# First batch of an attention and mixture kernel: second scores by blocks of 32 tokens, with the queries as the stationary side, and a new written order

## The chip, the core and the metric

The kernel runs on one core of a Trainium2 chip. TensorE multiplies (its weight loads are listed as PEld), VectorE (DVE), ScalarE (ACT) and GpSimd (POOL) work element by element, and SyncE (SP) issues the transfers. The metric is the device time in microseconds. The kernel before takes 466.59 us (median of 3 runs, 466.55 to 466.61).

## The reference

```python
batch, n_heads, seq, head_dim = (8, 8, 576, 64)      # p: 32 rows
def sm_attn(qq, kk, vv):
    s = scale * np.matmul(qq, kk.transpose(0, 1, 3, 2))
    s = s - np.max(s, axis=-1, keepdims=True)
    a = np.exp(s)
    a = a / (np.sum(a, axis=-1, keepdims=True) + 1e-09)
    return np.matmul(a, vv)
p_packed = sm_attn(p, k, v)
out = sm_attn(q, p_packed, p_packed)
...
h = np.maximum(np.maximum(x @ w1, x @ w2), x @ w3)
return (h @ w_out).astype(np.float32)
```

For every batch and head, 32 learned rows p attend to 576 keys (first scores); the 32 packed rows that come out are keys and values for the 576 queries (second scores, over 32 columns). The heads' outputs, side by side, are the tokens x of a layer with three 512 x 768 weights, a maximum over the three products, and a 768 x 512 output weight.

## The kernel before

The work of one batch is cut into steps named by a letter. `S` computes the first scores (`scores`), `A` their softmax and, for batches 0 and 1, the transposition on TensorE (`weigh_and_turn`), `Z` the inverse sums, `V` the values, `K` the packed rows, transposed into `pt_sb`, `Q` the second scores (`queries`), `B` their softmax (`attend`). From batch 2 on `X` (`spread`) stands for the transposition on TensorE: VectorE transposes 32 x 32 blocks (line 313), and 16 small transfers that SyncE issues (line 319) put the blocks in place. The packed rows aren't multiplied with the second softmax: `P` (`project`) multiplies them with the three weights of a group j of 128 columns, and `N` (`layer_in`) multiplies that with the softmax, which is layer 1. High and low parts of both operands, three products, stand in for full precision, so that one (j, half, weight) takes 6 matmuls of 288 columns. `E` takes the maximum over the weights, `H` prepares layer 2's operands, `O` is layer 2 (`layer_out`), `F` sums and stores. `k`, `v`, `q`, `w` are loads; `C` (`convert`) turns a weight block as it lies in memory into numbers: two steps on ScalarE (lines 188 and 193), a shift on VectorE (202), an addition on GpSimd (206). `W` prepares the output weight.

The order is written by hand, or by a program that printed it: the string `START` holds batches 0 and 1 and the beginning of batch 2, and the string `LOOP` one round for each batch from 2 on. Each word advances its step to the next `yield`; a last letter v, g or a moves that piece to VectorE, GpSimd or ScalarE. Each engine, SyncE too, takes its instructions in the order that the words give, and waits at one whose input isn't there. `I` and `J` are filler matmuls on an identity (`rouse`, line 143), by number of 128 columns.

Two heads share the 128 partitions of `q` (parities r = 0 and 1, 64 dimensions each), and a batch has four such pairs (`QUADS`). In `queries` the packed rows are stationary, so the scores come out with 32 packed rows of each pair as partitions and 288 tokens (a half, hf) as columns:

```python
nc.tensor.matmul(
    out=s2[b][hf][32 * n:32 * n + 32, r, 0:HS],
    lhsT=pt_sb[b % 2][o, NP * n:NP * n + NP], rhs=q[g][o, pr, hf * HS:(hf + 1) * HS],
```

`attend` therefore first transposes blocks of 32 x 32 on VectorE (line 389), so that a token's 32 scores lie in a row, then takes the maximum (393), subtracts (395), exponentiates (ScalarE, 397), sums (400), adds 1e-9 (403 or 405), inverts (407), multiplies (409), transposes back (412), and makes the high part (`a2h`, 415) and the low part (`a2l`, 418). In batch 0 it does so in four pieces of 288 columns, one for each parity and half (words `B000` to `B011`: batch, parity, half); later batches in two pieces of 576.

TensorE's tiles lie in PSUM: `ps_big` has two buffers of two banks (scores, projections), `ps_moe` four of one (layer 1, layer 2, filler). A buffer is given on when its last reader is done.

Of the kernel before, what the change touches and what calls it, by code (L numbers as in the profile page):

```python
# [10 lines left out]
F32 = mybir.dt.float32  # L11
# [21 lines left out]
NT = S // NP  # L33
# [55 lines left out]
def fused_kernel(ctx: ExitStack, tc: tile.TileContext, kp, qt, va, vb, wi, wo, out):  # L89
# [33 lines left out]
    def on(default):  # L123
        return engine[chosen[0] or default]
# [13 lines left out]
    def rouse(ps):  # L138

        k = ps.shape[-1] // P  # L140
        for i in range(0, idle[0], k):
            n = min(idle[0] - i, k)
            nc.tensor.matmul(  # L143
                out=ps[:, 0:n * P], lhsT=ident, rhs=ident.unsqueeze(1).to_broadcast([P, n, P]),
                start=True, stop=True,
            )
        idle[0] = 0
# [208 lines left out]
    def queries(b):  # L356

        q = [loaded["q", b, g] for g in range(G)]
        s2[b] = []
        for hf in range(2):  # L360
            s2[b].append(ps_big.tile([P, R, 512], F32, name=f"s2_{b}_{hf}", tag="big"))
            rouse(s2[b][hf][:, 0])
            for n, (g, pr) in enumerate(QUADS):
                for r in range(R):
                    o = slice(64 * r, 64 * r + 64)
                    nc.tensor.matmul(  # L366
                        out=s2[b][hf][32 * n:32 * n + 32, r, 0:HS],
                        lhsT=pt_sb[b % 2][o, NP * n:NP * n + NP], rhs=q[g][o, pr, hf * HS:(hf + 1) * HS],
                        start=True, stop=True,
                    )  # L370
            if b == 0 or hf == 1:
                yield 0

    def attend(b, r, hf=None):

        parts = range(2) if hf is None else (hf,)
        n = HS * len(parts)
        c = slice(parts[0] * HS, parts[0] * HS + n)
        nt = n // NP

        def buffer(name, dtype=F32):
            if (name, b, r) not in loaded:
                loaded[name, b, r] = pool.tile([P, S], dtype, name=f"{name}{b}_{r}", tag="y", bufs=NY)
            return loaded[name, b, r][:, c]


        e = buffer("e")
        for x in parts:
            nc.vector.transpose(out=e[:, x * HS - c.start:(x + 1) * HS - c.start], in_=s2[b][x][:, r, 0:HS])
        e3 = e.rearrange("p (t x) -> p t x", x=NP)  # L390
        yield 1
        m = pool.tile([P, nt], F32, name=f"m2_{b}_{r}_{c.start}", tag="m2", bufs=4)
        nc.vector.tensor_reduce(out=m, in_=e3, axis=AX.X, op=ALU.max)
        yield 0
        on("g").tensor_tensor(out=e3, in0=e3, in1=m.unsqueeze(2).to_broadcast([P, nt, NP]), op=ALU.subtract)
        yield 2
        nc.scalar.activation(out=e, in_=e, func=AF.Exp, scale=SCALE)
        yield 1
        z = pool.tile([P, nt], F32, name=f"z2_{b}_{r}_{c.start}", tag="z2", bufs=4)
        nc.vector.tensor_reduce(out=z, in_=e3, axis=AX.X, op=ALU.add)  # L400
        yield 0
        if on("a") is nc.scalar:
            nc.scalar.activation(out=z, in_=z, func=AF.Copy, bias=1e-9)
        else:
            nc.vector.tensor_scalar_add(out=z, in0=z, scalar1=1e-9)
        yield 0
        nc.vector.reciprocal(out=z, in_=z)
        yield 0
        on("v").tensor_tensor(out=e3, in0=e3, in1=z.unsqueeze(2).to_broadcast([P, nt, NP]), op=ALU.mult)
        yield 1  # L410
        et = buffer("et")
        nc.vector.transpose(out=et, in_=e)
# [6 lines left out]
        a2[b, r] = loaded["a2h", b, r], loaded["a2l", b, r]  # L419


    pw = {}
# [36 lines left out]
    def layer_in(b, j):  # L459

        p_hi, p_lo = pw[b, j]
        first = b == 0 and j == 0
        for hf in range(2):
            c = slice(hf * HS, (hf + 1) * HS)
            for i in range(NW):
                new = (range(NW) if i == 0 else ()) if first else (i,)
                for x in new:
                    sums[b, j, hf, x] = ps_moe.tile([P, 512], F32, name=f"mi{b}_{j}_{hf}_{x}", tag="moe")
                rouse(sums[b, j, hf, i])

                steps = [((2 * i + x) % 3, (2 * i + x) // 3) for x in range(2)] if first else [(i, 0), (i, 1)]
                for x, r in steps:
                    a_hi, a_lo = a2[b, r]
                    for n, (w, a) in enumerate(((p_hi, a_hi), (p_lo, a_hi), (p_hi, a_lo))):
                        nc.tensor.matmul(  # L475
                            out=sums[b, j, hf, x][:, 0:HS], lhsT=w[:, r, x * P:(x + 1) * P], rhs=a[:, c],
                            start=(r == 0 and n == 0), stop=(r == R - 1 and n == 2),
                        )
                yield 0
# [125 lines left out]
    def weigh_and_turn(b, r):  # L605
# [3 lines left out]


    stages = {
        "S": scores, "A": weigh_and_turn, "Z": invert, "X": spread, "V": lambda b, *rs: values(b, rs), "K": packed, "Q": queries,
        "B": attend, "C": convert, "P": project, "N": layer_in, "E": maximum, "H": halves,
        "O": layer_out, "F": finish, "W": weights,
    }
    loads = {"k": load_k, "v": load_v, "q": load_q, "w": load_w}
# [75 lines left out]
```

## Time and profile before

The table is from one profiled execution of the kernel before.

| | |
|---|---|
| median of the runs | 466.59 us |
| the profiled execution | 466.18 us |
| its span | 464.4 us |
| matmul instructions busy | 455.2 us (98%) |
| VectorE, GpSimd, ScalarE busy | 333.5, 247.9, 159.9 us |
| bytes read and written | 41.94 and 9.44 MB |

Lines of the chain of waits give a start, a length and what ran: `PE s L366` are the second scores, `PE s L253` the first, `PE mi L475` layer 1, `PE idle L143` filler, `DMA q<-in_qt` a load of q that was waited for. Rows of groups give busy time, mean ns of one, and the idle time before it with what ended it. Rows of a timeline give start, length, and how many instructions were merged. SPq is SyncE issuing. A matmul of plain 32-bit floats is two records. Matmul ends are modelled, so a busy matmul engine isn't one at its peak.

### The profile page before, as it was taken

The numbers are of one execution on the slowest core, as the hardware profiler recorded it, in microseconds if no ns is written. First come the engines' busy times: TensorE is split into PE (matmuls) and PEld (weight loads), VectorE is DVE, ScalarE is ACT, GpSimd is POOL, SyncE is SP. The second block draws the span as 40 slices with busy tenths as digits, with TensorE's granted clock in tenths as the row PEclk, the third lists the DMA queues.
The fourth block names the chain that finished last, engine by engine and source line by source line (L and its number), as shares of the span: only waits on it lengthen the run. The fifth ranks groups of instructions, "written<-read, shape, count | busy, mean of one in ns | idle before, by whom it ended". The sixth has DMA issues, their size and how long they took to land.

```text
span 464.4 us, 11561 instructions
## 1 busy us (share of the span) xinstructions
PE 455.2 (98%) x4724; PEld 404.9 (87%) x4724; DVE 333.5 (72%) x698; ACT 159.9 (34%) x341; POOL 247.9 (53%) x213
## 2 busy tenths in 40 slices
PE   7999998999999999999999999999999999999996
PEld 3477887899899898998899988998989988998996
DVE  1799987888887678566887479766786668845552
ACT  2787856535322126022331025121260223302130
POOL 0468875574542675526572384706764275725832
PEclk9999999999999999999999999999999999999999
DMA  8999846010316430256004450065202540020002
GB/s 313 398 382 355 321 98 230 1 58 25 95 66 195 135 119 1 80 160 233 2 27 152 87 211 2 27 199 155 94 1 94 151 116 1 28 76 1 2 6 97
DMA packets 35780, 55.66 MB, mean 120 GB/s; under 512 B 17296, under 2 KB 26512, under 8 KB 35728
## 3 DMA queue, kind: packets, MB, share of 16 engines
q1 hardware_dynamic: 35728, 54.93, 35.4%
q8 instruction: 37, 0.61, 0.5%
q14 instruction: 15, 0.12, 0.1%
HBM read 41.94 MB, written 9.44 MB: 111 GB/s over the span
## 4 chain that ended last, share of the span: by engine, by line
PE 88%; DMA 5%; SPq 3%; DVE 3%; issue 1%; ACT 1%; DVEq 0%
PE mi L475 44%; PE mo L544 29%; PE pw L439 6%; PE idle L143 2%; SPq L319 2%; PE s L366 2%; PE av L337 2%; DMA wi<-in_wi 2%; PE s L253 2%; DMA q<-in_qt 1%; DMA kt<-in_kp 1%; PE tp L296 0%; DMA xt<-x 0%; SPq L159 0%; PE pa L337 0%
## 5 line engine op out<-in xcount | busy, mean ns | idle before, releaser
L475 PE MATMUL mi<-a2h,ph 128*128 128x288 f32 x576 | 173.5, 301 | 0.8 <-DVE pl L452 0.6
L475 PE MATMUL mi<-a2l,ph 128*128 128x288 f32 x576 | 169.9, 295 | 0.0
L475 PE MATMUL mi<-a2h,pl 128*128 128x288 f32 x576 | 169.6, 295 | 0.0
L489 DVE TENSOR_TENSOR r<-mi,r 128x288 f32<-128x288 f32 x192 | 84.4, 452 | 57.8 <-PE mi L475 55.3
L475 PEld LDWEIGHTS mi<-a2h,ph 128*128 128x128 f32 x576 | 108.0, 188 | 13.4 <-issue 7.0
L475 PEld LDWEIGHTS mi<-a2l,ph 128*128 128x128 f32 x576 | 108.0, 188 | 0.2
L475 PEld LDWEIGHTS mi<-a2h,pl 128*128 128x128 f32 x576 | 108.1, 188 | 0.0
L513 POOL TENSOR_TENSOR r<-r 128x288 f32<-128x288 f32 (+1 forms) x47 | 50.4, 1083 | 81.3 <-DVE r L489 65.5
L129 ACT COPY r<-mi 128x288 f32<-128x288 f32 x73 | 29.0, 399 | 185.8 <-PE mi L475 185.7
L450 ACT ACTIVATE ph<-pw 128x384 fp32r<-128x384 f32 (+1 forms) x67 | 40.2, 631 | 46.5 <-PE pw L439 43.5
L452 DVE SCALAR_TENSOR_TENSOR pl<-pw,ph 128x384 fp32r<-128x384 f32 (+1 forms) x67 | 46.2, 713 | 9.5 <-ACT ph L450 9.2
L544 PE MATMUL mo<-ych,xl 128*128 128x288 f32 x144 | 42.5, 295 | 0.0
L544 PE MATMUL mo<-ych,xh 128*128 128x288 f32 x144 | 42.4, 294 | 0.0
L544 PE MATMUL mo<-ycl,xh 128*128 128x288 f32 x144 | 42.3, 294 | 0.0
L439 PE MATMUL pw<-w_sb,pt 64*32 64x384 f32 x768 | 36.3, 487 | 0.1
L206 POOL TENSOR_TENSOR w_sb<-w_sb,wi 128x512 int32<-128x512 int32 x18 | 23.9, 1336 | 22.0 <-DVE w_sb L202 17.4
L134 POOL TENSOR_TENSOR ybl<-r,ybh 128x576 fp32r<-128x576 f32 x15 | 21.7, 1448 | 19.7 <-DVE ybh L131 16.2
L134 POOL TENSOR_TENSOR ycl<-r,ych 128x864 fp32r<-128x864 f32 x12 | 26.6, 2218 | 5.1 <-PE mi L475 2.4
L544 PE MATMUL mo<-yah,xh 128*128 128x288 f32 x96 | 28.9, 301 | 0.0
L544 PE MATMUL mo<-yal,xh 128*128 128x288 f32 x96 | 28.4, 296 | 0.2 <-DVE yal L134 0.2
L544 PE MATMUL mo<-ybh,xh 128*128 128x288 f32 x96 | 28.3, 295 | 0.0
L544 PE MATMUL mo<-yah,xl 128*128 128x288 f32 x96 | 28.3, 295 | 0.0
(123 smaller groups left out, 808.4 us busy)
## 6 DMA issues: line engine op xcount, KB each, us to landing
kt<-in_kp SPq DMA_DIRECT2D x16, 640.0 KB, 5.4
q<-in_qt SPq DMA_DIRECT2D x16, 576.0 KB, 5.6
wi<-in_wi SPq DMA_DIRECT2D x18, 512.0 KB, 8.6
v<-in_va SPq DMA_DIRECT2D x16, 512.0 KB, 5.7
wi<-in_wo SPq DMA_DIRECT2D x6, 512.0 KB, 6.7
out_t<-r SPq DMA_DIRECT2D x8, 288.0 KB, 2.2
out_t<-t SPq DMA_DIRECT2D x8, 288.0 KB, 2.3
out_t<-s SPq DMA_DIRECT2D x8, 288.0 KB, 2.7
```

The costliest lines, as they stand in the source:

```text
L129: e.copy(out=out, in_=src)
L134: on(default).tensor_tensor(out=lo, in0=src, in1=hi.bitcast(F32), op=ALU.subtract)
L143: nc.tensor.matmul(out=ps[:, 0:n * P], lhsT=ident, rhs=ident.unsqueeze(1).to_broadcast([P, n, P]), start=True, stop=True,)
L206: nc.gpsimd.tensor_tensor(out=dst.bitcast(I32), in0=dst.bitcast(I32), in1=up, op=ALU.add)
L253: nc.tensor.matmul(out=s1[b][r][32 * n:32 * n + 32, hf, 0:HS], lhsT=kt[g][o, w:w + NP], rhs=kt[g][o, pr * S + hf * HS:pr * S + (hf + 1) * HS],
L439: nc.tensor.matmul(out=ps[r][NP * n:NP * n + NP, 0:NW * P], lhsT=pt_sb[b % 2][o, NP * n:NP * n + NP], rhs=w_sb[o, j, n * NW * P:(n + 1) * ...
L450: nc.scalar.activation(out=hi[:, r], in_=x, func=AF.Copy, scale=2.0 ** -WS)
L452: nc.vector.scalar_tensor_tensor(out=lo[:, r], in0=x, scalar=2.0 ** -WS, in1=hi[:, r].bitcast(F32), op0=ALU.mult, op1=ALU.subtract,)
L475: nc.tensor.matmul(out=sums[b, j, hf, x][:, 0:HS], lhsT=w[:, r, x * P:(x + 1) * P], rhs=a[:, c], start=(r == 0 and n == 0), stop=(r == R - ...
L489: nc.vector.tensor_tensor(out=h, in0=sums[b, j, hf, i][:, 0:HS], in1=h, op=ALU.max)
L513: less = lambda out, x, y: on("g").tensor_tensor(out=out, in0=x, in1=y, op=ALU.subtract)
L544: nc.tensor.matmul(out=ps[:, 0:HS], lhsT=w[:, x, m * P:(m + 1) * P], rhs=h[:, z], start=(p == 0 and i == 0), stop=(p == NQ - 1 and i == 2),)
```

## The change

Only batch 0's second scores and their softmax change in what they do, and `START` is another order of the same words but for these.

`queries_by_token` takes 32 tokens of q as the stationary side and the 32 packed rows as the moving side, for every block of 32 tokens: 9 blocks, 4 pairs and 2 parities in each half, 144 matmuls in place of 16. A token's 32 scores lie in a row at once. `attend_half` takes one half of the tokens with both parities: the maximum and the subtraction read PSUM, on VectorE, with nothing transposed ahead; from the exponential on it shares the steps with the other batches (`softmax`). Batch 0 has two pieces of 576 columns in place of four of 288.

```diff
+    def queries_by_token(b):
...
+        for hf in range(2):
+            s2[b].append(ps_big.tile([P, R, 512], F32, name=f"s2_{b}_{hf}", tag="big"))
+            rouse(s2[b][hf][:, 0])
+            for t in range(HS // NP):
+                for n, (g, pr) in enumerate(QUADS):
+                    for r in range(R):
+                        o = slice(64 * r, 64 * r + 64)
+                        c = hf * HS + t * NP
+                        nc.tensor.matmul(
+                            out=s2[b][hf][NP * n:NP * n + NP, r, t * NP:(t + 1) * NP],
+                            lhsT=q[g][o, pr, c:c + NP], rhs=pt_sb[b % 2][o, NP * n:NP * n + NP],
+                            start=True, stop=True,
+                        )
+            yield 0
...
+    def attend_half(hf):
...
+        nc.vector.tensor_reduce(out=m, in_=src, axis=AX.X, op=ALU.max)
+        yield 0
+        e = buffer("e", F32)
+        nc.vector.tensor_tensor(
+            out=e.rearrange("p (r t x) -> p r t x", r=R, x=NP), in0=src,
+            in1=m.unsqueeze(3).to_broadcast([P, R, NT // 2, NP]), op=ALU.subtract,
+        )
+        yield 0
+        z = pool.tile([P, NT], F32, name=f"z2_0_{hf}", tag="z2", bufs=4)
+        hi, lo = yield from softmax(e, z, buffer)
...
 START = """
-k00 k01 I10 S0 A00 A00 J9 A00 q00 A00 w00 A01 A01 v00 J6 A01 v01 Z01 C00 C00 Z00 w02 C02 A01v V00 C00 V00 q01
...
+w12 k01 k00 C12 C12 w01 C01 w00 J17 I10 S0 v00 w02 A01 A01 J9 A01 v01 q00 C00 C00 C00 A00 A00 Z01 C02 C02 C00
+q01 C02 Z00 A01v J9 A00 C02 V01 C01 C01 A00 V00 C01 V00 w11 w10 V01 J2 K0 C11 C12 K0v C12 J2 Q0 C11 C11 B00 Q0
...
```

Lines behind line 142 have a number lower by one in the new kernel, and higher by 34 or 35 from `pw` on. Three places of the new order follow, before and after.

SyncE, the first transfers of the program; kt, q and v are batch 0's loads (the digit is the pair group), wi0_2 is block 2 of weight group 0. Before:

```order
L159 DMA kt0_79<-in_kp 128x1280
L159 DMA kt1_81<-in_kp 128x1280
L174 DMA q0_122<-in_qt 128x1152
L153 DMA wi0_0_127<-in_wi 128x512
L165 DMA v0_136<-in_va 128x1024
L166 DMA v0_136<-in_vb 64x256
L165 DMA v1_149<-in_va 128x1024
L166 DMA v1_149<-in_vb 64x256
L153 DMA wi0_2_160<-in_wi 128x512
L174 DMA q1_189<-in_qt 128x1152
L153 DMA wi0_1_216<-in_wi 128x512
```

After:

```order
L152 DMA wi1_2_79<-in_wi 128x512
L158 DMA kt1_81<-in_kp 128x1280
L158 DMA kt0_83<-in_kp 128x1280
L152 DMA wi0_1_87<-in_wi 128x512
L152 DMA wi0_0_90<-in_wi 128x512
L164 DMA v0_119<-in_va 128x1024
L165 DMA v0_119<-in_vb 64x256
L152 DMA wi0_2_122<-in_wi 128x512
L164 DMA v1_142<-in_va 128x1024
L165 DMA v1_142<-in_vb 64x256
L173 DMA q0_145<-in_qt 128x1152
L173 DMA q1_163<-in_qt 128x1152
```

A block of weight group 1 stands ahead of the keys, and four weight blocks in place of two ahead of the second q.

VectorE, from batch 0's second scores on (s2 the scores, m2 the maxima, e0 the exponentials, w_sb the converted weights). Before:

```order
L389 STREAM_TRANSPOSE e0_1_234<-s2_0_0_225 128x288
L393 TENSOR_REDUCE m2_0_1_0_237<-e0_1_234 128x9
L395 TENSOR_TENSOR e0_1_234<-e0_1_234,m2_0_1_0_237 128x288
L202 TENSOR_SCALAR w_sb_72<-wi0_1_216 128x512
L389 STREAM_TRANSPOSE e0_0_260<-s2_0_1_248 128x288
L389 STREAM_TRANSPOSE e0_0_260<-s2_0_0_225 128x288
L393 TENSOR_REDUCE m2_0_0_288_263<-e0_0_260 128x9
L393 TENSOR_REDUCE m2_0_0_0_265<-e0_0_260 128x9
L395 TENSOR_TENSOR e0_0_260<-e0_0_260,m2_0_0_288_263 128x288
L395 TENSOR_TENSOR e0_0_260<-e0_0_260,m2_0_0_0_265 128x288
```

After:

```order
L201 TENSOR_SCALAR w_sb_72<-wi1_1_233 128x512
L424 TENSOR_REDUCE m2_0_0_322<-s2_0_0_247 128x18
L427 TENSOR_TENSOR e0_0_397<-s2_0_0_247,m2_0_0_322 128x576
L201 TENSOR_SCALAR w_sb_72<-wi1_0_235 128x512
L424 TENSOR_REDUCE m2_0_1_403<-s2_0_1_324 128x18
L397 TENSOR_REDUCE z2_0_0_405<-e0_0_397 128x18
L427 TENSOR_TENSOR e0_1_410<-s2_0_1_324,m2_0_1_403 128x576
L404 RECIPROCAL z2_0_0_405<-z2_0_0_405 128x18
L406 TENSOR_TENSOR e0_0_397<-e0_0_397,z2_0_0_405 128x576
L409 STREAM_TRANSPOSE et0_0_414<-e0_0_397 128x576
L487 SCALAR_TENSOR_TENSOR pl0_1_436<-pw0_1_426,ph0_1_435 128x768
L487 SCALAR_TENSOR_TENSOR pl0_0_474<-pw0_0_0_439,ph0_0_473 128x384
```

A weight block that is loaded behind the second q is converted first; half 1's maximum stands ahead of half 0's sum, and half 1's subtraction ahead of half 0's reciprocal.

VectorE, up to batch 2's block transposes of line 313 (x2 the tile that they fill, r0 the maxima of layer 1, mx2 and z2 maxima and sums). Before:

```order
L489 TENSOR_TENSOR r0_1_705<-mi0_2_1_1_725,r0_1_705 128x288
L202 TENSOR_SCALAR w_sb_72<-wi5_2_580 128x512
L202 TENSOR_SCALAR w_sb_72<-wi4_2_733 128x512
L266 TENSOR_REDUCE mx2_0_797<-s1_2_0_740 128x1
L267 TENSOR_SCALAR nm2_0_798<-mx2_0_797 128x1
L266 TENSOR_REDUCE mx2_1_804<-s1_2_1_741 128x1
L267 TENSOR_SCALAR nm2_1_805<-mx2_1_804 128x1
L400 TENSOR_REDUCE z2_1_1_0_816<-e1_1_630 128x18
L313 STREAM_TRANSPOSE x2_820<-a1_2_0_801 128x18x32
L313 STREAM_TRANSPOSE x2_820<-a1_2_1_808 128x18x32
```

After:

```order
L201 TENSOR_SCALAR w_sb_72<-wi4_0_792 128x512
L265 TENSOR_REDUCE mx2_1_893<-s1_2_1_826 128x1
L266 TENSOR_SCALAR nm2_1_894<-mx2_1_893 128x1
L404 RECIPROCAL z2_1_1_859<-z2_1_1_859 128x18
L397 TENSOR_REDUCE z2_1_0_861<-e1_0_703 128x18
L523 TENSOR_TENSOR r0_1_809<-mi0_3_0_1_850,r0_1_809 128x288
L523 TENSOR_TENSOR r0_1_809<-mi0_3_0_2_864,r0_1_809 128x288
L312 STREAM_TRANSPOSE x2_947<-a1_2_0_897 128x18x32
L312 STREAM_TRANSPOSE x2_947<-a1_2_1_902 128x18x32
```

A reciprocal and two layer-1 maxima now stand between batch 2's softmax maxima and the transposes. SyncE's order from there is as before: the 16 small transfers, two output-weight blocks, the two q blocks of batch 2.

More of the change, by code (lines that the diff above doesn't have):

```diff
@@ new lines @@
+q01 C02 Z00 A01v J9 A00 C02 V01 C01 C01 A00 V00 C01 V00 w11 w10 V01 J2 K0 C11 C12 K0v C12 J2 Q0 C11 C11 B00 Q0
+B00 C10 C10 C10 C11 B01 B00 C10 B00 B00 B01 B00 B00 B00 v11 B00g k10 J7 P01 P01 P01 P00 B00 k11 J4 S1 P00 P00
+N00 B01 B01 B01v A10 B01 w31 N01 P00 P00 N00 A11 C31 B01g C31 C31 N00 A10 E000v E000 B01 E000 w32 C32 Z10 A11
+w20 w22 C20 A10 A10 N01 C31 C32 v10 B01g A11 A11 C20 w21 N01 C20 q10 B01v C21 C32 V101 N01 N01 q11 Z11 C32 w30
+C20 E010v E010 E010 C22 C22 V101 K1 N00 C21 C21 C21 C22 E011v K1 Q1 B10 N00 C22 P02 B11 w52 C30 B11 C30 C30
@@ new lines @@
+C30 w42 B10 P10 B10 P02 P02 E011 N00 N01 E001 k21 k20 E001 E001 C52 w41 P10 B11 C42 C42 P03 E011 P10 w40 w50
+P03 P03 C52 C52 N02 E020 N02 N02 S2 N03 N03 C42 C42 B11 B10 E020 N03 C41 C40 C41 B11 B11 N02 C40 A20 E030v
+E020 C41 C40 E021 A21 A20 w60 A21 w51 N02 v20 N02 C52 C60 C51 C41 B11 B10 E030 v21 P11 E030 C50 C40 H00 X2 X2
+B11g P04 P04 N03 N03 C50 C50 w64 E021 E031 N03 P04 N04 w61 E031 Z20 C51 C50 C51 H00 E040 B10v N04 B10 B11 C51
+B11 X2 E040 N04 E021 P05 N04 E031 P05 E040 H01 C60 B10g Z21 E041 B10 B11 H02 P05 N04 N04 N05 E050 P11 E041
@@ new lines @@
+B10g E041 H04 N05 E050 N05 w65 w63 B10v H00v P11 C61 C61 C61 H03 H01 N05 C60 N10 N05 E050 V201 C60 N11 N11 C65
+N11 E051v q20 N10 H03 V201 q21 E051 E110 E110 C64 E100v E100 w62 C61 N11 E111 K2 K2 H02v H02 H04 E110 N11 C64
+N05 E051 Q2 E111 B20 B21 C62 N10 N10 E101 C65 C65 H01 W0 H01v N11 P12 W0v W0v C64 H04v P13 P12 E111 P13 W0 H03
+P12 N10 N10 E101 C64 P13 N12 H03v W0v W0 P15 C63 C62 C62 P14 N12 E120 C63 H05 N12 N12 P14 E120 E101 E121 C63
+P14 P15 N12 N12 E120 E121 E121 E100 C65 C62 N13 N13 E130v B21 E130 N13 N14 C63 N14 W1 W1v W1v W1 H05v W0 N14
@@ new lines @@
+W0v W2v W2v N14 N13 N14 E140 E140 W1v W1 E130 E141 N13 E141 N14 E131 W2 W2 H01 P15 N15 N15 E150 N15 W1 N15
+E141 N15 B21 H12 H10v W1 E151 H05 E131 E150 B20 E140 N15 W0v W2v k31 H03 W0 O0 O0 W2 E151 H05v W1v N13 k30 F0
+W2v F0 E151 O0 H11 H05 W1 O0 O0 O0 H03 B21 B20v F0 W2 E131 H01v F0 F0 H05v O0 F0 O0 O0 O0 B21 H13 H14v F0 P22
+B20 W2 H12 W2 H12 B20 F0 H10 H13v H10v H13v P20 P20 P21 F0 F0 B20 O0 F0 E150 O0 O0 H11v P20 P20 P20 O0 F0 F0
+H13v F0 H14 H14v P22 O1 F1 H15v H15v H11 H11v O1 O1 F0 O1 O1 P21 O1 H15v H15v H15v B21v H13 H13v H11 H11v H15v
@@ L73 @@
+O1 F1 F1 B21 F1 F1 O1 P22 O1 O1 F1 B20 B21g B20 F1 O1 B21 B21g F1 F1 F0 O1 O1 F1 F1 P21 B20 F1 F1 F1 B20v B20v
+F1 B21v O1 F1
 """
@@ L370, in queries, with softmax @@
                     )
-            if b == 0 or hf == 1:
+            if hf == 1:
                 yield 0
[L374 to L389, printed above, removed]
-        e3 = e.rearrange("p (t x) -> p t x", x=NP)
[L391 to L396, printed above, removed]
+    def queries_by_token(b):
+        q = [loaded["q", b, g] for g in range(G)]
+        s2[b] = []
+        for hf in range(2):
[12 more added lines that the diff above has]
+            yield 0
+    def softmax(e, z, buffer):
+        e3 = e.rearrange("p (t x) -> p t x", x=NP)
         nc.scalar.activation(out=e, in_=e, func=AF.Exp, scale=SCALE)
         yield 1
-        z = pool.tile([P, nt], F32, name=f"z2_{b}_{r}_{c.start}", tag="z2", bufs=4)
         nc.vector.tensor_reduce(out=z, in_=e3, axis=AX.X, op=ALU.add)
@@ L408, in attend @@
         yield 0
-        on("v").tensor_tensor(out=e3, in0=e3, in1=z.unsqueeze(2).to_broadcast([P, nt, NP]), op=ALU.mult)
+        on("v").tensor_tensor(out=e3, in0=e3, in1=z.unsqueeze(2).to_broadcast([P, NT, NP]), op=ALU.mult)
         yield 1
-        et = buffer("et")
+        et = buffer("et", F32)
         nc.vector.transpose(out=et, in_=e)
@@ L418, in attend @@
         split_lo(lo, et, hi)
-        a2[b, r] = loaded["a2h", b, r], loaded["a2l", b, r]
+        return hi, lo
+    def attend_half(hf):
+        src = s2[0][hf][:, :, 0:HS].rearrange("p r (t x) -> p r t x", x=NP)
+        buffer = lambda name, dtype: pool.tile([P, S], dtype, name=f"{name}0_{hf}", tag="y", bufs=NY)
+        m = pool.tile([P, R, NT // 2], F32, name=f"m2_0_{hf}", tag="m2", bufs=4)
+        nc.vector.tensor_reduce(out=m, in_=src, axis=AX.X, op=ALU.max)
[8 more added lines that the diff above has]
+        hi, lo = yield from softmax(e, z, buffer)
+        for r in range(R):
+            a2[0, r, hf] = [x[:, r * HS:(r + 1) * HS] for x in (hi, lo)]
+    def attend(b, r):
+        buffer = lambda name, dtype: pool.tile([P, S], dtype, name=f"{name}{b}_{r}", tag="y", bufs=NY)
+        e = buffer("e", F32)
+        e3 = e.rearrange("p (t x) -> p t x", x=NP)
+        for hf in range(2):
+            nc.vector.transpose(out=e[:, hf * HS:(hf + 1) * HS], in_=s2[b][hf][:, r, 0:HS])
+        yield 0
+        m = pool.tile([P, NT], F32, name=f"m2_{b}_{r}", tag="m2", bufs=4)
+        nc.vector.tensor_reduce(out=m, in_=e3, axis=AX.X, op=ALU.max)
+        yield 0
+        on("g").tensor_tensor(out=e3, in0=e3, in1=m.unsqueeze(2).to_broadcast([P, NT, NP]), op=ALU.subtract)
+        yield 0
+        z = pool.tile([P, NT], F32, name=f"z2_{b}_{r}", tag="z2", bufs=4)
+        hi, lo = yield from softmax(e, z, buffer)
+        for hf in range(2):
+            a2[b, r, hf] = [x[:, hf * HS:(hf + 1) * HS] for x in (hi, lo)]
     pw = {}
@@ L472, in layer_in @@
                 for x, r in steps:
-                    a_hi, a_lo = a2[b, r]
+                    a_hi, a_lo = a2[b, r, hf]
                     for n, (w, a) in enumerate(((p_hi, a_hi), (p_lo, a_hi), (p_hi, a_lo))):
                         nc.tensor.matmul(
-                            out=sums[b, j, hf, x][:, 0:HS], lhsT=w[:, r, x * P:(x + 1) * P], rhs=a[:, c],
+                            out=sums[b, j, hf, x][:, 0:HS], lhsT=w[:, r, x * P:(x + 1) * P], rhs=a,
                             start=(r == 0 and n == 0), stop=(r == R - 1 and n == 2),
@@ L611, in fused_kernel @@
     stages = {
-        "S": scores, "A": weigh_and_turn, "Z": invert, "X": spread, "V": lambda b, *rs: values(b, rs), "K": packed, "Q": queries,
-        "B": attend, "C": convert, "P": project, "N": layer_in, "E": maximum, "H": halves,
+        "S": scores, "A": weigh_and_turn, "Z": invert, "X": spread, "V": lambda b, *rs: values(b, rs), "K": packed, "Q": lambda b: queries(b) if b else queries_by_token(b),
+        "B": lambda b, x: attend(b, x) if b else attend_half(x), "C": convert, "P": project, "N": layer_in, "E": maximum, "H": halves,
         "O": layer_out, "F": finish, "W": weights,
```

24 lines of the change are left out of this document (removed).

## The prediction

> **What bounds the kernel now.** I read the page first, then the chain of waits, then TensorE's waits, then the timeline of SyncE and VectorE in the first 70 us. The page: the matmul engine is busy through almost the whole span, filler matmuls included.
>
> ```profile
> span 464.4 us, 11561 instructions
> PE 455.2 (98%) x4724; PEld 404.9 (87%) x4724; DVE 333.5 (72%) x698; ACT 159.9 (34%) x341; POOL 247.9 (53%) x213
> ```
>
> The chain of waits says where the real work begins and where it halts (start, length, what):
>
> ```profile
> 7.16 1.17 PE s L253 x24
> ...
> 16.26 1.16 PE s L366 x32
> ...
> 26.94 1.92 PE mi L475 x12
> 28.86 0.43 PE idle L143 x2
> 29.29 1.13 PE s L253 x32
> ...
> 65.49 1.93 DMA xt<-x
> ...
> 69.49 6.43 DMA q<-in_qt
> ...
> 76.06 1.21 PE s L366 x32
> ```
>
> The first layer-1 matmul (mi) starts at 26.94. From there TensorE has real work without a break but for two waits of the first 110 us (total, times, longest):
>
> ```profile
> PE s L366 <- DMA q<-in_qt: 1.3, 1, 1.3
> ...
> PE mi L475 <- DVE r L489: 0.3, 1, 0.3
> ```
>
> So the time is: when the dense stretch begins, plus a fixed amount of matmul work, plus these two waits, 1.6 us together. The change touches the stretch before 26.94 and the order up to the loop. Batches 2 to 7 have the same instructions. The first wait belongs to the second scores of batch 2 at 76.06: their q comes last in a series that SyncE issues one by one.
>
> ```profile
> 54.84 11.26 SPq L319 DMA_DIRECT2D xt<-x  x16
> 66.20 1.01 SPq L153 DMA_DIRECT2D wi<-in_wo  x2
> 68.93 0.88 SPq L174 DMA_DIRECT2D q<-in_qt  x2
> ```
>
> Sixteen small transfers take 11.26 us to issue; two weight blocks and the two q blocks follow; the second q lands at 69.49 + 6.43 = 75.92, and TensorE starts at 76.06. Whatever moves 54.84 moves 76.06.
>
> **The change part by part.** *The loads.* These rows give a transfer's issue and its time to landing, for the second q, and for two weight blocks behind it.
>
> ```profile
> 7.13 0.33 SPq L174 DMA_DIRECT2D q<-in_qt  x1
> q<-in_qt SPq DMA_DIRECT2D x1, 576.0 KB, 9.1
> ```
>
> ```profile
> 10.05 0.33 SPq L153 DMA_DIRECT2D wi<-in_wi  x1
> wi<-in_wi SPq DMA_DIRECT2D x1, 512.0 KB, 9.1
> ```
>
> ```profile
> 11.53 0.33 SPq L153 DMA_DIRECT2D wi<-in_wi  x1
> wi<-in_wi SPq DMA_DIRECT2D x1, 512.0 KB, 8.9
> ```
>
> ```profile
> kt<-in_kp SPq DMA_DIRECT2D x16, 640.0 KB, 5.4
> ...
> v<-in_va SPq DMA_DIRECT2D x16, 512.0 KB, 5.7
> ```
>
> The second q lands at 16.2 now, just when the second scores start. Landings follow the sum of what was asked before. Up to the second q the new order asks 4 weight blocks, 2 k, 2 v with their tails of 64 KB and 2 q: 2048 + 1280 + 1152 + 1152 = 5632 KB. The old order had asked 5632 KB with the block issued at 10.05, which landed at 19.2. So the second scores can't start before about 19.2, 2.9 us later than 16.26. The keys come 512 KB later, which by (19.2 - 16.2) / 2 is 1.5 us; the first scores then start at 8.7, and with the old distance of 9.1 us (7.16 to 16.26) the second would at 17.8. VectorE's new wait for a weight block between the two maxima (both maxima, two exponentials and the second transpose are queued behind it) is covered by the remaining 1.4 us; without that cover it costs its length.
>
> *The second scores.* 144 matmuls in place of 16, recorded as 288 in place of 32, with the same 9216 streamed columns in all. The floor is therefore the 1.16 us of the old row. The nearest rows for many short matmuls on 32-column strips are those of the values:
>
> ```profile
> 159.48 1.39 PE av L337 x80
> ```
>
> ```profile
> 159.41 1.10 PE L337 MATMUL av<-v,xt 128*32 128x64 f32 x64
> ```
>
> That is 1.39 / 80 = 17.4 ns a record with its breaks, and, when the last record's own length (about 0.22, by the row below) is taken off, (1.10 - 0.22) / 63 = 14.0 ns in the steady run.
>
> ```profile
> L337 PE MATMUL av<-v,xt x80: 216/219/243, 159.4 to 160.7; 128*32 128x64 f32 x64, 64*32 64x64 f32 x16
> ```
>
> Bounds: 1.2 to 288 x 17.4 = 5.0 us. I take 14.0, thus 4.0 us: half 0 at 21.2, half 1 at 23.2. [...]
>
> *The softmax of half 0.* Prices by row (busy, mean ns), on VectorE, then ScalarE, then GpSimd:
>
> ```profile
> L266 DVE TENSOR_REDUCE mx<-s 128x1 f32<-128x576 f32 x16 | 12.0, 752 | 11.6 <-PE s L253 11.6
> L412 DVE STREAM_TRANSPOSE et<-e 128x576 f32<-128x576 f32 x14 | 10.7, 765 | 0.0
> L202 DVE TENSOR_SCALAR w_sb<-wi 128x512 uint32<-128x512 uint32 x18 | 8.5, 484 | 0.2
> L395 DVE TENSOR_TENSOR e<-e,m 128x576 f32<-128x576 f32 x7 | 8.2, 1167 | 0.2
> L409 DVE TENSOR_TENSOR e<-e,z 128x576 f32<-128x576 f32 x5 | 3.9, 788 | 0.2
> L407 DVE RECIPROCAL z<-z 128x18 f32<-128x18 f32 x14 | 3.5, 254 | 2.5 <-ACT z L403 2.5
> ```
>
> ```profile
> L188 ACT ACTIVATE wi<-wi 128x512 f32<-128x512 f32 x24 | 16.3, 684 | 10.9 <-DMA wi<-in_wo 7.1 <-DMA wi<-in_wi 3.5
> ```
>
> ```profile
> L134 POOL TENSOR_TENSOR a2l<-et,a2h 128x576 fp32r<-128x576 f32 x8 | 11.4, 1431 | 0.5
> L131 POOL CAST a2h<-et 128x576 fp32r<-128x576 f32 x11 | 7.7, 703 | 3.0 <-PE mo L544 2.3 <-DVE et L412 0.7
> ```
>
> VectorE's first new row is a weight block that lands right behind the second q, at 11.53 + 8.9 = 20.4. ScalarE 0.68, VectorE about 0.45: 21.6, so half 0 of the scores (21.2) is hidden. Maximum 0.75: 22.3. Subtraction out of PSUM: no row has it; between 0.75 (a 576-wide row that reads PSUM) and 1.17 (the subtraction out of SBUF). I take 0.75, the row that shares its source: 23.1. Behind it stand the next weight block (0.45) and half 1's maximum (0.75), longer than the exponential beside them: 24.3. Sum 0.75, half 1's subtraction 0.75, reciprocal 0.25: 26.1. Product 0.79, transposition 0.77: 27.6. GpSimd 0.70 and 1.43: 29.7, of which two matmuls come before the low part. These durations overlap at their ends by some hundredths each, so I take 29.4 for the first layer-1 matmul in dense order.
>
> *What that is worth.* The new order has batch 1's first scores (1.13) before this point, and not the filler of 0.43; the old kernel was as far at 26.94 + 0.43 + 1.13 = 28.50. The dense stretch is 0.9 us late. The removed transposes and the merged steps free VectorE, but its first row waits for a load.
>
> *Up to batch 2's q.* VectorE's rows in the old trace, from batch 1's transposes on:
>
> ```profile
> 39.72 1.72 DVE L389 STREAM_TRANSPOSE e<-s 128x288 f32<-128x288 f32 x4
> ...
> 43.91 1.67 DVE L489 TENSOR_TENSOR r<-mi,r 128x288 f32<-128x288 f32 x4
> ...
> 53.35 1.42 DVE L313 STREAM_TRANSPOSE x<-a 128x576 f32<-128x576 f32 x2
> ```
>
> From 39.72 to the end of the x transposes at 54.77 are 15.05 us without a break worth naming, 23 rows between the two. The new order has 26 there: one maximum (1.67 / 4 = 0.42), one copy of the same size and one reciprocal (0.25) more, 1.1 us. So the x transposes end at 39.72 + 0.9 + 15.05 + 1.1 = 56.8, 2.0 us later, and the q of batch 2 lands at 75.92 + 2.0 = 77.9. Batch 2's second scores now stand behind 12 more layer-1 matmuls (258 for 246), 12 x 3.47 / 24 = 1.7 us by the row below. TensorE would come to them at 76.06 - 1.3 + 1.7 + 0.9 = 77.4 and waits until 78.0. The old kernel was as far at 77.8. Net +0.2.
>
> ```profile
> 92.26 3.47 PE mi L475 x24
> ```
>
> *Behind that* layer 2 begins 72 matmuls later than it did, so the 0.3 us wait for a maximum probably goes: -0.3. **Sum: -0.1 us.** The profiled execution took 466.18 us (464.4 span, 1.8 around it), the median of the runs is 466.59; on the median I forecast 466.5. A measurement of this kernel can tell about 0.2%, 0.9 us, from no change.
>
> **The rivals.** *1, faster: the q of batch 2 comes in time.* If VectorE reaches the x transposes no later than 55.7 (work between the two places is hidden in gaps that I count as full) and the dense stretch begins at 28.9, the q lands by 76.9 and TensorE, there at 76.9, hardly waits: -0.9, and the 0.3 behind it: 465.4. For it: every small wait between 27 and 55 in the new order is one that the old one had too. Against: the old VectorE rows stand end to end.
>
> *2, slower: short matmuls cost by the piece.* Half 1's maximum stands on VectorE ahead of half 0's sum, and starts at 23.5 if the scores are ready. That is the point from which it decides: 4.3 us for 288 records, 14.9 ns each. At the 17.4 ns of the row with breaks, half 1 is ready at 24.2: +0.7. With a cost between that and the old records' 1.16 / 32 = 36 ns, say 27 ns, it is ready at 27.0: +3.5, which goes through to the end: 470.0. For it: no row has 32 columns. Against: records of different strips start 14.0 ns apart with twice the columns. [...]
>
> *3, slower: the new subtraction costs 1.17 as from SBUF.* Both halves' subtractions stand in the chain to the first layer-1 matmul: +0.8, passed on to the x transposes: 467.3, and 467.6 if the 0.3 wait stays.
>
> **How the numbers follow.** The forecast (dense start 29 to 30, q landing near 78) has a chance of 0.44, rival 1 0.26, rival 2 0.17, rival 3 and other slips on VectorE 0.13. The range: rival 1 with half a microsecond more below, 465.0; rival 2 at about 22 ns above, 469.0. Faster by over 0.2%: 0.26; within: 0.44; slower: 0.30.
>
> **What would show it.** Right: second scores of batch 0 start at 19 to 19.5 and take about 4 us; first layer-1 matmul near 29.4 behind batch 1's first scores; the x transfers start at 56 to 57.5; TensorE waits for q once, under 1 us; loop batches as before. Wrong: a q that lands by 17.5, second scores of over 5 us or under 2, a new wait of over 1 us in the dense stretch, or a layer-2 stretch with waits of its own.

## The result and the profile after

The changed kernel takes 476.63 us (median of 4 runs, 475.57 to 477.29), the kernel before in the same session 466.57 us. The ratio is 1.0215, 95% interval 1.0202 to 1.0229: 10.06 us slower, where 466.5 was forecast and 469.0 was the upper end.

The page of the changed kernel: span, the matmul engine, and the TensorE clock that was granted in 40 slices of 11.9 us.

```profile
span 474.8 us, 12058 instructions
PE 459.7 (97%) x4978; PEld 408.4 (86%) x4978; DVE 333.1 (70%) x684; ACT 159.6 (34%) x335; POOL 244.4 (51%) x209
...
PEclk9959999999999999999999999999999999999999
```

One slice, from 23.7 to 35.6 us, has half the clock. The chain of waits says what happens there, and that the loop is as it was (first scores at 206.00 and 260.03, 54.03 apart). The changed kernel:

```profile
22.18 3.04 issue
...
26.77 4.63 issue
...
39.37 3.54 PE mi L509 x24
...
206.00 1.13 PE s L252 x32
...
260.03 1.13 PE s L252 x32
```

The kernel before, the same two rounds, 54.02 apart:

```profile
195.77 1.13 PE s L253 x32
...
249.79 1.13 PE s L253 x32
```

So the loss stands ahead of the loop: both rounds come 10.2 us later. The new second scores (L385) stop twice, for 3.04 and 4.63 us, in "issue": TensorE waits for nothing that the profile shows. The dense part, layer 1 with hardly a break, begins at 39.37 in the chain (39.30 in the timeline, whose rows overlap a little). The old kernel was as far at 28.50, so it is 10.9 us late instead of 0.9. TensorE's timeline of that stretch counts the records between the stops:

```profile
21.40 0.77 PE L385 MATMUL s<-pt,q 64*32 64x32 f32 x66
25.21 1.56 PE L385 MATMUL s<-pt,q 64*32 64x32 f32 x128 [3.04 <-issue]
31.41 1.19 PE L385 MATMUL s<-pt,q 64*32 64x32 f32 x94 [4.63 <-issue]
32.53 2.87 PE L142 MATMUL idle<-ident 128*128 128x512 f32 x4
```

128 records between two stops, each with a weight load of its own (PEld): 256 instructions. Now the rows for DMA queues, which the prediction had passed over; in the page of the kernel before, then of the changed kernel (packets, MB, share):

```profile
q8 instruction: 37, 0.61, 0.5%
```

```profile
q8 instruction: 39, 0.64, 0.6%
```

0.61 MB / 37 is 16 KB a packet. The kernel before has 2 x 4724 = 9448 matmuls and weight loads, which by the 256 between the stops is 9448 / 256 = 36.9 pieces; the changed one has 2 x 4978 = 9956, and 38.9. So the packets are by their number TensorE's code, which comes over the DMA engines in pieces of 16 KB, 256 instructions (16 KB / 256 = 64 bytes each, an estimate). Both boundaries inside the short matmuls, behind 66 and 194 of the 288 records, have a stop.

During the second stop this moved on the DMA engines (from 26.77 to 31.41):

```profile
q1 hardware_dynamic: 558, 1.81, 102.9%
q8 instruction: 1, 0.02, 1.5%
```

One packet of code, among 1.81 MB of loads that keep the engines full. This is the **code theory**: a piece is asked for when TensorE enters the one before it; with the loads under way it is there some 6 us later; long matmuls take longer than that over 256 instructions (24 records of layer 1 take 3.54 us above, so 128 would take 18.9, an estimate), and 128 of the short ones take 1.6 us. From the end of the first stop (the second piece is entered at 25.21) to the end of the second (31.41) are 6.20 us. That the entry is what asks for the piece is inferred from such distances; no view shows the asking. Against the code theory stand the **piece-price theory**, that short matmuls with a new stationary side stop by themselves, and the **order theory**, that the new order is late whatever the form of the scores.

### The profile page after: what moved, and what is told of

The parts are those of the page before. It is cut to its first block, busy times and chain, and to the rows that moved or that the text cites. A ratio compares the mean times of both kernels' runs of the same rounds, so it can differ in the third digit from the quotient of the medians.

```text
span 474.8 us, 12058 instructions
## 1 busy us (share of the span) xinstructions
PE 459.7 (97%) x4978; PEld 408.4 (86%) x4978; DVE 333.1 (70%) x684; ACT 159.6 (34%) x335; POOL 244.4 (51%) x209
## 4 chain that ended last, share of the span: by engine, by line
PE 92%; DMA 3%; issue 2%; DVE 1%; SPq 0%; ACT 0%; DVEq 0%
PE mi L509 49%; PE mo L578 28%; PE pw L474 7%; DMA wi<-in_wi 3%; PE av L336 2%; PE s L252 2%; PE s L365 2%; PE idle L142 1%; PE s L385 1%; DVE a2l L133 0%; PE tp L336 0%; PE av L351 0%; PE tp L295 0%; SPq L158 0%; SPq L152 0%
## 5 line engine op out<-in xcount | busy, mean ns | idle before, releaser
L547 POOL TENSOR_TENSOR r<-r 128x288 f32<-128x288 f32 (+1 forms) x50 | 52.2, 1055 | 83.8 <-DVE r L523 67.7
L205 POOL TENSOR_TENSOR w_sb<-w_sb,wi 128x512 int32<-128x512 int32 x18 | 23.5, 1313 | 29.1 <-ACT wi L192 15.0
L133 POOL TENSOR_TENSOR ycl<-r,ych 128x864 fp32r<-128x864 f32 x13 | 29.3, 2250 | 5.2 <-PE mi L509 3.9
L133 POOL TENSOR_TENSOR ybl<-r,ybh 128x576 fp32r<-128x576 f32 x14 | 20.0, 1426 | 16.5 <-DVE ybh L130 16.1
L578 PE MATMUL mo<-ybh,xl 128*128 128x288 f32 x96 | 28.3, 295 | 0.0
```

The lines of the kernel that those rows point to most:

```text
L133: on(default).tensor_tensor(out=lo, in0=src, in1=hi.bitcast(F32), op=ALU.subtract)
L205: nc.gpsimd.tensor_tensor(out=dst.bitcast(I32), in0=dst.bitcast(I32), in1=up, op=ALU.add)
L547: less = lambda out, x, y: on("g").tensor_tensor(out=out, in0=x, in1=y, op=ALU.subtract)
L578: nc.tensor.matmul(out=ps[:, 0:HS], lhsT=w[:, x, m * P:(m + 1) * P], rhs=h[:, z], start=(p == 0 and i == 0), stop=(p == NQ - 1 and i == 2),)
```

## The experiments

### Old form of the scores in the new order

```diff
-  "Q": lambda b: queries(b) if b else queries_by_token(b)
+  "Q": queries
   # attend_half, ahead of the maximum:
+  for r in range(R):
+      nc.vector.transpose(out=e[:, r * HS:(r + 1) * HS], in_=s2[0][hf][:, r, 0:HS])
```

> The changed kernel with batch 0's second scores computed the old way (32 records with the packed rows stationary, four 32 x 32 transposes on VectorE ahead of the maxima), in the new order and with both parities in one softmax step. Code theory (TensorE's instructions arrive in pieces of 256; a piece is asked for when the one before it is entered and is there 6.2 to 6.6 us later while the loads run; the two breaks in the second scores, 3.04 and 4.63 us, are waits for that): no break over 0.5 us in the second scores, which run from about 21.4 to 22.6; VectorE then needs 2.4 us more than in the changed kernel, and dense layer 1 begins at about 33 instead of 39.3, so the time is near 470 (469 to 471.5). Order theory (the new order is late by itself, whatever the form of the scores): 475 or more. Piece-price theory (short matmuls with a new stationary side stop by themselves): as the code theory, about 470.

468.65 us (467.86 to 468.89), ratio 1.0035 (1.0022 to 1.0049). TensorE's timeline, where dense layer 1 begins at 31.25:

```profile
20.58 1.20 PE L365 MATMUL s<-q,pt 64*32 64x288 f32 x32
...
31.25 0.40 PE L512 MATMUL mi<-a2h,ph 128*128 128x288 f32 x1
```

No stop in the scores, and some 8 of the 10 us gone, somewhat more than expected (the dense part was expected near 33). The order theory can have at most 1.9 us.

### Loads held back

```diff
+  def hold(hf):          # SyncE waits for half 0's maximum
+      nc.sync.dma_start(out=t, in_=held[hf])
-  B00 v11 B00g
+  B00 D0 v11 B00g
```

> The changed kernel, with SyncE made to wait for half 0's maximum (a transfer of that small tile) before it asks for the loads from batch 1's second v on, so that little else is under way while the second scores run. Code theory: a piece of code is there 2.5 to 4 us after it is asked for instead of 6.2 to 6.6; the first break shrinks from 3.0 to under 1, the second from 4.6 to about 1; half 1 is done near 26.5 instead of 32.5 and the time is 470 to 471.5, if no held load comes too late. Piece-price theory: both breaks stay, 475 or more. Order theory: no change or slower, since loads only come later.

473.42 us (472.62 to 475.38), ratio 1.0146 (1.0119 to 1.0172). TensorE's timeline, and the DMA engines between the two ends of the stops:

```profile
22.01 1.31 PE L385 MATMUL s<-pt,q 64*32 64x32 f32 x128 [0.76 <-issue]
25.46 1.06 PE L385 MATMUL s<-pt,q 64*32 64x32 f32 x94 [2.15 <-issue]
```

```profile
q1 hardware_dynamic: 144, 0.01, 2.7%
q8 instruction: 1, 0.02, 2.1%
```

The stops stand at the same records and are 0.76 and 2.15 long instead of 3.04 and 4.63. With next to nothing else on the engines a piece takes 25.46 - 22.01 = 3.45 us, against 6.20. So the loads make nearly half of a piece's time, and 4.8 of the 7.7 us of the stops; the rest stays even without them. The packet itself takes 1.1 us in both kernels; what the loads delay is its start, which comes, by narrow windows of the DMA view, 3.7 us after the piece before it is entered (28.94) in the changed kernel and 1.1 us after (23.14) here. By the piece-price theory both stops would have stayed as they were. The gain is smaller than expected, by some 2 to 3 us. The dense part starts at 34.59, 4.7 us earlier, but TensorE now waits behind that for a held v (0.6; ahead of it 0.3 for a k), and the rounds of the loop, at 202.36 and 256.57, are 54.21 apart instead of 54.03, about 1.1 us in six rounds. What makes them longer stays open.

### The new scores added to the old kernel

```diff
+  def unused(b):         # the 144 new matmuls, into tiles that nothing reads
-  ... Q0 w12 ... C12 J11 P00
+  ... Q0 D0 w12 ... C12 P00
```

> The kernel before, with the new second scores of batch 0 computed as well, behind the old ones, into tiles that nothing reads (288 records more), in the place of a filler of 11 units. Code theory: the added records break off twice, at a distance of 128 records; the first break ends near 19.5, the second near 25.8; the first projection comes at about 27.3 instead of 19.98, layer 1 begins about 3 us late, time 469 to 470.5. Piece-price theory with the 12 ns per record that the changed kernel shows in its runs without a break: 3.5 us in a place where TensorE idles or fills for 2.6 us, and again for 4.7 us behind: 466.4 to 467. The order is the old one, so the order theory gives 466.4 to 467 too.

478.67 us (477.54 to 479.28), ratio 1.0244 (1.0224 to 1.0264).

```profile
16.53 0.68 PE L384 MATMUL unused<-pt,q 64*32 64x32 f32 x47
18.69 1.28 PE L384 MATMUL unused<-pt,q 64*32 64x32 f32 x128 [1.48 <-issue]
24.88 1.38 PE L384 MATMUL unused<-pt,q 64*32 64x32 f32 x109 [4.92 <-issue]
...
31.08 0.80 PE L456 MATMUL pw<-w_sb,pt 64*32 64x384 f32 x1 [3.47 <-issue]
```

The two stops are where the code theory had them, 128 records apart, and in the old order. The expected size was too small by 8 us and more: there is a third boundary, in the last record of the first projection (L456), which is a long matmul. The three stops are 9.9 us, and the filler behind them takes 7.61 us at a lower clock (0.50 granted from 24 to 36, 0.81 from 36 to 40), 4.78 in the kernel before, at 1.00; layer 1 begins at 40.15 instead of 26.87 (timeline). The stop belongs to the boundary and not to the short matmul; the short ones only bring it too early. 24.88 - 18.69 and 31.08 - 24.88 are 6.19 and 6.20, the same time as in the changed kernel.

### Fewer of them

```diff
-  for hf in range(2): for t in range(HS // NP):
+  for hf in range(1): for t in range(5):
```

> The kernel before with 40 of the 144 new matmuls added (80 records, 160 instructions) where the earlier run had all of them, unused. Code theory: one break, again behind 47 records (the boundary of 256 stands in the program, not in the form of the matmul), of 1.2 to 1.7 us, ending near 18.7; the other 33 records end near 19.2, before the first projection at 19.98; the next boundary comes behind enough long matmuls. Time 466.4 to 467. A theory in which short matmuls themselves stop after a while (some limit of the matmul engine) puts the stop at 66 or 128 records or not at all.

468.0 us (467.06 to 470.12), ratio 1.0043 (1.0025 to 1.0060).

```profile
16.89 0.68 PE L384 MATMUL unused<-pt,q 64*32 64x32 f32 x47
19.19 0.40 PE L384 MATMUL unused<-pt,q 64*32 64x32 f32 x33 [1.62 <-issue]
```

One stop behind 47 records again, with 33 records to come instead of 241. Place, number and length are as expected, the time is not: about 1 us more than the upper end. Layer 1 begins half a microsecond later than in the old kernel, and TensorE's list of waits has 0.8 us for the x transfers and 0.4 for a v, which the old kernel doesn't wait for. The remainder stays open.

### The boundary moved

```diff
-  w00 J17 I10 S0
+  w00 T17 J14 I10 S0     # T: tiny matmuls on the identity
```

> The changed kernel with 17 tiny matmuls (34 records, 68 instructions) ahead of the first scores, and three units of filler less. Code theory: the places of the breaks move 34 records forward, to records 32 and 160 of the 288; the piece before the first is entered at about 15.4 instead of 18.6, so the first break nearly goes (under 1 us); half 0 is complete before the second break, near 23.5 instead of 26.8; the second break is 4 to 5 us and half 1 ends near 29.8 instead of 32.5; time about 473.8 (473 to 475). Piece-price theory: breaks at the same records as before (66 and 194), time 476.6. Order theory: 476.6.

481.6 us (481.31 to 482.6), ratio 1.0318 (1.0301 to 1.0336).

```profile
22.02 0.46 PE L385 MATMUL s<-pt,q 64*32 64x32 f32 x34
23.38 1.28 PE L385 MATMUL s<-pt,q 64*32 64x32 f32 x128 [0.90 <-issue]
29.58 1.52 PE L385 MATMUL s<-pt,q 64*32 64x32 f32 x126 [4.92 <-issue]
...
34.68 1.44 PE L142 MATMUL idle<-ident 128*128 128x384 f32 x2 [1.57 <-issue]
```

34 records added less one filler of 2 records moved the boundary by 32, from 66 to 34, and shortened the first stop to 0.90. That settles the place: it goes by the number of instructions, and not by the form of the matmuls. The time went the other way, 5.0 us up instead of 2.8 down. Half 1 comes earlier, but the shift brings a third boundary into the filler ahead of the first projection, which the expectation had not counted, and the dense part starts at 40.98, 1.7 us later than in the changed kernel. Further on loads come onto the path that were hidden: a v that SyncE waits for delays the x transfers (a line of the chain), and TensorE waits for these (a line of its waits), which it does not in the changed kernel. What is left of the 5.0 is not followed up.

```profile
159.34 6.18 DMA v<-in_va
...
PE av L336 <- DMA xt<-x: 2.2, 3, 1.6
```

### The change without its code

The old 32 records, and the new softmax steps on them as they lie. This kernel leaves out the four transposes, so that the softmax runs over another axis; it serves for the time alone.

```diff
   # in the first experiment's kernel
-  for r in range(R): nc.vector.transpose(...)
```

> The changed kernel without the code: batch 0's second scores by the old 32 records, and the new softmax step on them as they lie, without the four transposes (so the softmax runs over the wrong axis; all durations stay). It has what the prediction assumed, except that the scores take 1.1 us and not 3.5. Code theory (only the waits for instructions are missing from the prediction): the first layer-1 matmul of the dense order starts at 29.4 to 29.8, and the time is 466.5 to 467.2 (466.5 by the prediction's sum, 467.0 from the run with old scores, 468.65, less 1.68 us of transposes). Order theory (the new order has a lateness of its own beyond the breaks, as the 1.9 us of the run with old scores could mean): dense start over 30.5, time 468 or more.

466.93 us (465.89 to 468.06), before in the same session 466.11; ratio 1.0012 (0.9997 to 1.0028): not to be told from the old kernel, as forecast. TensorE, then VectorE:

```profile
20.72 1.21 PE L365 MATMUL s<-q,pt 64*32 64x288 f32 x32
...
29.55 0.40 PE L509 MATMUL mi<-a2h,ph 128*128 128x288 f32 x1
```

```profile
22.66 0.76 DVE L427 TENSOR_TENSOR e<-s,m 128x576 f32<-128x576 f32 x1
...
23.67 0.75 DVE L424 TENSOR_REDUCE m<-s 128x18 f32<-128x576 f32 x1
```

The dense part starts at 29.55; 29.4 was forecast. The order theory falls: of the 1.9 us that it had left in the first experiment, 1.7 go with the four transposes (468.65 to 466.93).

### The same with a shorter filler

```diff
-  w00 J17 I10 S0
+  w00 J8 I6 S0
```

> The run above with a shorter filler ahead of the first scores (14 units of 128 columns for 27). If the filler sets the start of the first scores (10.38 in the changed kernel, where the prediction had 8.7), they start 2 to 3 us earlier, near 7.5 to 8, and the second scores 1 to 2 us earlier, bounded by the second q at about 17.7. If the weight block behind the second q (w11, there at 20.2) holds VectorE as the prediction had it, the dense start does not move by more than 0.3 us and the time stays within 0.5 us of the run above. If instead the first scores set the dense start, the time falls by 1 to 2 us, to 465 to 466.

467.58 us (466.67 to 468.94), ratio 1.0032 (1.0019 to 1.0046). TensorE, then VectorE:

```profile
18.80 1.21 PE L365 MATMUL s<-q,pt 64*32 64x288 f32 x32
...
24.54 1.56 PE L474 MATMUL pw<-w_sb,pt 64*32 64x384 f32 x32 [2.83 <-POOL w_sb L205]
...
29.75 0.40 PE L509 MATMUL mi<-a2h,ph 128*128 128x288 f32 x1
```

```profile
22.60 0.43 DVE L201 TENSOR_SCALAR w_sb<-wi 128x512 uint32<-128x512 uint32 x1 [0.53 <-ACT wi L187]
```

The first scores start at 7.78, where they now wait for the keys, and the second 1.9 us earlier than in the run above (20.72), but the dense part does not. VectorE's row between the two maxima waits for the weight block, and half 1's maximum comes only 0.7 earlier (22.94); the first projection waits 2.83 us for the same block on GpSimd and comes 0.7 earlier too (24.54 for 25.21). These 0.7 are lost again behind it, where the filler takes 2.07 us instead of 1.13. So the weight block covers 1.2 of the 1.9 us in this run. The time, 0.65 us above the run above, lies just outside the 0.5 that was expected; why is open.

### What else is in the 10 us

VectorE's row for half 1's maximum in the changed kernel:

```profile
32.64 0.76 DVE L424 TENSOR_REDUCE m<-s 128x18 f32<-128x576 f32 x1 [4.45 <-PE s L385]
```

From there to the dense part are 39.37 - 32.64 = 6.7 us; the run without the code has 29.55 - 23.67 = 5.9. The fillers in between run at half the clock (0.50 granted from 32 to 34; four records in 2.87 us, 1.77 in the run without the code), and the projection behind them is late: VectorE's low part of it (pl) waits for ScalarE's high part (ph), which it does not in the run without the code.

```profile
37.16 1.42 DVE L487 SCALAR_TENSOR_TENSOR pl<-pw,ph 128x768 fp32r<-128x768 f32 x2 [0.65 <-ACT ph L485]
```

Two runs leave the fillers out:

```diff
-  B00g k10 J7 P01 ... k11 J4 S1
+  B00g k10 P01 ... k11 S1
```

> The changed kernel without the two fillers between the second scores and the dense part (7 and 4 units). After the second break these 4 + 2 matmuls run at half the clock (starts 0.85 us apart instead of 0.43) and stand ahead of the first projection (35.33) and of batch 1's first scores (37.83). If they are on the path, as the 0.8 us by which the dense start is later than half 1's maximum explains suggest, the dense start moves from 39.3 to 38.0 to 38.6 and the time falls to 475.4 to 476. If VectorE and GpSimd set the dense start (low part of the softmax done at 38.7), or if the projection and the first scores now run cold in the filler's place, nothing is gained: 476.4 to 477.2. Code theory and the theories against it agree on this run; it settles what beside the breaks is in the 10 us.

> The changed kernel with both: SyncE held until half 0's maximum, and the two fillers left out. Code theory: the breaks are as in the run with the hold alone (0.8 and 2.2 us by the list of waits), the dense start 33.5 to 34.3 instead of 34.6, the time 472.4 to 473.4. It is the best that these edits leave of the new form of the scores, and still slower than the kernel before, since two boundaries of 256 instructions always fall into 576.

477.52 us (475.88 to 479.4; ratio 1.0217, 1.0188 to 1.0246), and with the loads held as well 476.19 us (473.32 to 477.36; ratio 1.0191, 1.0153 to 1.0229). No gain in either (the hold alone had 473.42), and both times lie above what was expected, the second by 2.8 us; the runs scatter too much for tenths. In both, TensorE then waits for pl ahead of batch 1's first scores, 0.9 and 2.6 us. Stretches of 4 us (PE, PEld, DVE, ACT and POOL busy, granted clock, DMA share, GB/s), of the changed kernel and of the one without the fillers:

```profile
20.00:24.00 4.00, 2.12 (x72) 1.26 (x72) 2.38 (x5) 1.50 (x3) 3.09 (x3) 1.00 1.04 378
24.00:28.00 4.00, 1.56 (x128) 1.43 (x128) 1.66 (x3) 0.11 (x1) 0.04 (x1) 0.57 1.02 407
...
32.00:36.00 4.00, 4.00 (x80) 1.98 (x75) 3.29 (x6) 0.22 (x1) 0.00 (x0) 0.65 0.65 210
36.00:40.00 4.00, 4.00 (x63) 1.86 (x48) 3.29 (x6) 3.29 (x6) 2.08 (x2) 1.00 0.02 6
```

```profile
32.00:36.00 4.00, 2.53 (x34) 0.65 (x18) 3.93 (x7) 3.00 (x7) 0.53 (x1) 0.83 0.64 207
36.00:40.00 4.00, 3.69 (x38) 2.57 (x39) 3.44 (x9) 1.25 (x4) 2.14 (x3) 0.60 0.26 47
```

With the stops the granted clock is down to 0.50; in the run without the code it is 1.00 in every stretch from 20 to 44. Shorter windows of the same view of the changed kernel have it at 1.00 up to 24.5, so that it falls within the first stop, and at 1.00 again from 35 on. With the fillers TensorE works on without a gap, at 1.00 from 36 to 40; without them it idles again (2.53 of 4 us busy), and the dense part starts earlier, at 38.03, but on 0.60 of the clock from 36 to 40.

## Why the prediction was wrong

**The step that failed** is the second scores: "I take 14.0, thus 4.0 us: half 0 at 21.2, half 1 at 23.2", with bounds of 1.2 to 5.0. They took from 21.40 to 32.60, 11.2 us, and with that the prediction's own sign of being wrong was there, second scores of over 5 us. Without the two stops they are 3.5 us. The price of a record was good, even high: with a record's own length of 0.24 taken off, 66 records in 0.77 us at a clock of 1.00 are (0.77 - 0.24) / 65 = 8.2 ns, and 128 in 1.56 at 0.50 are (1.56 - 0.24) / 127 = 10.4 ns. What lacked was a term: the delivery of 576 instructions, which the sum put at nothing. It is 7.7 us in TensorE's waits:

```profile
PE s L385 <- issue: 7.7, 2, 4.6
...
PE mi L509 <- DVE a2l L133: 0.3, 1, 0.3
```

The bounds came from rows of 80 records, 160 instructions, in which no such wait stands; a row shorter than a piece of 256 instructions can't bound the 576 here.

**The other steps.**

- *Loads and start of the second scores* (19.2): the second q, asked for at 8.76, lands 8.9 us later, at 17.7, earlier than forecast, so the sum of what was asked before does not by itself give a landing. The first scores stand behind a filler that I had not added up, and start at 10.38 and not at 8.7; the second start at 21.40. With the old 32 records that hardly counts: the cover that the prediction named, the weight block that VectorE waits for, holds for 1.2 of the 1.9 us that the shorter filler gains. With the new records it counts: without the 7.7 us of stops half 1's maximum (32.64) would stand at 24.9, an estimate, 1.4 behind the 23.5 of the prediction. The transfer, by its issue in the changed kernel:

```profile
q<-in_qt SPq DMA_DIRECT2D x1, 576.0 KB, 8.9
```

- *Softmax* (dense part at 29.4): right, 29.55 without the code. The subtraction out of PSUM takes 0.76, so rival 3 falls. That TensorE is there at the same time was luck: its first projection waits 1.6 us for the weight block on GpSimd, and the filler and the first scores behind that end at 29.6, a path that the prediction didn't have.
- *Batch 2's q* (a net +0.2 with a wait of 0.6): too pessimistic. In the run without the code SyncE begins the x transfers at 56.45, 1.6 us later than before (2.0 forecast), but asks for q only 0.8 later (68.93 before), and TensorE doesn't wait for it, in that run or in the changed kernel. The old wait of 1.3 us is gone, as in rival 1.

```profile
56.45 11.85 SPq L318 DMA_DIRECT2D xt<-x  x16
...
69.74 2.30 SPq L173 DMA_DIRECT2D q<-in_qt  x2
```

- *The wait of 0.3 for a maximum*: gone, as forecast; a new one of 0.3 for a low part (above) takes its place.
- *Rival 2* had the effect (half 1 late, from there to the end) without the cause: it sought it in the price of each record, whose condition, more than 14.9 ns, isn't met. (By its own sum 22 ns would give 468.5 and not 469.0; nothing here hangs on that.)

The sum: 10.9 us late at the dense part, less 1.3 and 0.3 for the waits that went, plus 0.3 for the new one, are 9.6; the spans of the two profiled executions differ by 10.4 (474.8 and 464.4). The missing 0.8 have a visible place that the prediction didn't have. A projection of 48 records ahead of batch 3's first scores takes 3.00 us instead of 2.17, since a weight load in it waits for VectorE. Before, then after:

```profile
122.70 2.17 PE L439 MATMUL pw<-w_sb,pt 64*32 64x384 f32 x48
```

```profile
127.08 3.00 PE L474 MATMUL pw<-w_sb,pt 64*32 64x384 f32 x48
128.56 0.18 PEld L474 LDWEIGHTS pw<-w_sb,pt 64*32 64x32 f32 x16 [0.70 <-DVE v L597]
```

The run without the code has the same projection in the same two pieces (in the chain 18 records in 1.41 us and 30 in 1.52), which is why its span, 465.1, is not below the old one. Smaller differences are not followed up.

In the 10.9 are the 0.9 of the forecast, 9.1 by which half 1's maximum (32.64) is later than its 23.5, and 0.8 behind it, where the clock is low. Of the 9.1, 7.7 are the stops and 1.4, by the estimate above, the late start of the scores. That the 0.8 come from the fillers at half the clock is argued and not shown, since leaving them out moved the dense part but not the time.

None of the versions here beats the kernel before.

## What to carry to other kernels

Count the instructions where a change makes many of few: matmuls and weight loads, here in pieces of 256. Where 256 of them ran in less time than a piece needed to come (1.3 to 1.6 us, against 6.2 under full loads and 3.45 without), TensorE waited at every boundary inside them, though a record cost only 8.2 to 10.4 ns. The page of the kernel before shows the pieces already, in the instruction row of its DMA queues (37 packets). The bound taken from rows of 160 instructions (1.2 to 5.0 us) did not hold for the 576 here, which took 11.2.

## What the runs showed of the hardware

- A piece of TensorE's code took 6.19 to 6.20 us from boundary to boundary in three kernels with the DMA engines full (the changed one, the new scores added to the old one, the run without fillers; DMA share 1.01 to 1.04), and 3.45 with them nearly empty (2.7%, loads held). Its packet took 1.1 us in the changed kernel and with the loads held; it started 3.7 us behind the boundary in the first and 1.1 in the second.
- In a row of stops of 3.04 and 4.63 us the granted clock went from 1.00 to 0.50 within the first (at 24.5); it was back at 1.00 from 35 on, some 3.5 us after TensorE had gone on without a gap (31.41). Behind stops of 0.76 and 2.15 us, in the run with the loads held, the four filler records took 3.27 us, against 1.77 in the run without the code.
- The place of a boundary went by the number of instructions ahead of it, to the record: 32 records more ahead moved it by 32, from 66 to 34.
